# Half of the layer norms offered to GpSimd, and a planner with other transfer times

## The chip, the cores and the metric

The kernel runs on one core of a Trainium2 chip. Its time is the device time of one execution in microseconds (us); several runs give a median. A core has five engines that run their own instruction queues side by side and meet through semaphores: TensorE (PE in the profile, its weight loads PEld), VectorE (DVE), ScalarE (ACT), GpSimd (POOL) and SyncE (SP), which here issues nearly all DMAs.

## The reference, cut to what matters

Two layers, each an attention with a compressive memory (A) and a feed-forward part (B), over 2048 tokens of 640 features in bfloat16. Both layers use the same weights.

```python
def _layernorm(x, axis=-1, eps=1e-05):
    m = jnp.mean(x, axis=axis, keepdims=True)
    v = jnp.var(x, axis=axis, keepdims=True)
    return (x - m) / jnp.sqrt(v + eps)
...
        for s in range(N):                       # N = 4 segments of 512 tokens, H = 32 heads of 20
            qs, ks, vs = (q[:, :, s].copy(), k[:, :, s].copy(), v[:, :, s].copy())
            logits = jnp.einsum('bhqd,bhkd->bhqk', qs, ks) * scale + mask
            p = _softmax(logits, axis=-1)
            a_dot = jnp.einsum('bhqk,bhkd->bhqd', p, vs)
            pq = phi(qs)
            num = jnp.einsum('bhld,bhde->bhle', pq, M)
            den = jnp.einsum('bhld,bhd->bhl', pq, z)[..., None] + 1e-06
            o = g * (num / den) + (1.0 - g) * a_dot
            outs.append(o)
            pk = phi(ks)
            M = M + jnp.einsum('bhld,bhle->bhde', pk, vs)
            z = z + jnp.einsum('bhld->bhd', pk)
...
    x = x + _A_ref(_layernorm(x, axis=-1), A_wq, A_wk, A_wv, A_wo, A_beta)
    x = x + _B_ref(_layernorm(x, axis=-1), B_w1, B_w2)   # relu(x w1) w2, 1728 wide
    x = x + _A_ref(_layernorm(x, axis=-1), A_wq, A_wk, A_wv, A_wo, A_beta)
    x = x + _B_ref(_layernorm(x, axis=-1), B_w1, B_w2)
```

## The kernel before

The residual x stays on the chip (`x_sb`, 16 tiles of 128 tokens). The work is cut by layer a and segment s of four token tiles, written (a,s). For each segment: statistics of each tile on VectorE (`stats`, L729 and L731), variance to reciprocal root on GpSimd (`chain`, the `pow` at L745), the norm itself, which subtracts the mean and multiplies (L775, 128 x 640 to `xn_tok`, two tiles to a slot), and a DMA transposition of each slot (`turn`, L751) to `xnT`. From it K and Q (`proj_part`), V (`proj_v`) or the hidden layer of the feed-forward part (`ffn`) are multiplied by `group`, whose matmuls stand at L708 (128 columns of weights at a time) or L711 (the same as four quarters of 32 columns side by side).

K and Q go through a scratch in DRAM (`spill`, L998, written once, and `fill`, L1042, read as `pad`, with heads spread over rows). The scores of two head groups take five rounds of matmuls (L1226), ScalarE takes their exponentials to `PT` (L1288), GpSimd cuts the part above the diagonal to zero (L1300, the masks), and TensorE multiplies by V (L1320, the value products; L1359 for two of the 64 head groups). The result is cast to `otu`, transposed, divided, added to the memory's part, transposed again to `oT` and multiplied by wo (`out_proj`). The memory itself is written (`mem_write`, L1163) from `phk`, the transposed phi of K, and read at L1106. In the end the sums of the last feed-forward tiles are stored (L1574, L1578).

Nothing of the order is written out by hand. The pieces are generators (streams) that yield operations. A planner, `Sched.run`, keeps a modelled free time for each engine; at each step it takes the stream whose next operation can start first, and records it in its engine's queue. An operation that names two engines goes to the one on which it would end first, as `evac` does for ScalarE and VectorE. The planner's costs are written into the helpers: `dve`, `act`, `pool` for compute, and `issue`, `lat`, `rate` and `holds` for a DMA (the queue's time, time to landing, bytes per ns, and whether SP is taken to stand still until the transfer is done). `SHIFT` moves the modelled start of single pieces, named by stream number and segment, forward or back in that comparison, in ns. None of these numbers is executed: they decide only the order of the queues, and which of two engines gets an operation. The recorded queues are in-order on every engine.

TensorE's array is used in three forms: the full 128 x 128, in four quarters by columns (L711, L1320, L1500) and in four by rows (the scores, L1226). The planner chooses between full and quarters for the operations that offer both, by what stands next to them.

Of the kernel before, what the change touches and what calls it, by code (L numbers as in the profile page):

```python
# [7 lines left out]
ALU = mybir.AluOpType  # L8
# [151 lines left out]
class Spawn:  # L160
# [13 lines left out]
PE_MARGIN = 80.0  # L174
HOLDERS = 1
SHIFT = {
# [8 lines left out]
}  # L185
HOLD_TOL = {"pe": 220.0, "act": 150.0, "dve": 200.0, "pool": 0.0, "sp": 0.0}

# [248 lines left out]
               ("dve", 66.0 + n / (0.96 * mode), [(vfn, True)], 95.0)], waits, urgent=True)  # L436


def pool(ns, fn, waits=()):
    return Op([("pool", ns, [(fn, True)], 60.0)], waits)  # L440

# [7 lines left out]
def bass_interleave_layers__memory_aug_infini_attn__dense_activation_relu__prompt_kernel(  # L449
    nc, A_x, A_wq, A_wk, A_wv, A_wo, A_beta, B_x, B_w1, B_w2, out,  # L450
):
    with contextlib.ExitStack() as es:
# [120 lines left out]
        def late_loads():  # L573

            def x_pieces(s):
                def one(t):
                    return lambda e: e.dma_start(x_sb[:, t, :], xs[:, t, :])
                return [("x%d" % s, 163840, one(4 * s + i)) for i in range(4)]

            def rows(name, w, src, k):  # L580
                return (name, 163840, lambda e: e.dma_start(w[:, k, :], src[128 * k:128 * k + 128, :]))

            def half(k, h):
                cs = slice(h * (DFF // 2), (h + 1) * (DFF // 2))
                return ("w1%d" % h, 221184, lambda e: e.dma_start(w1_r[:, k, cs], B_w1[128 * k:128 * k + 128, cs]))

            pieces = x_pieces(2)
            pieces += [rows("wo", wo_r, A_wo, k) for k in range(FC)]
            pieces += x_pieces(3)
            pieces += [half(k, h) for h in range(2) for k in range(FC)]  # L590
            n2 = len(pieces)
            pieces += [rows("w2", w2_r, B_w2, k) for k in range(NFULL)]
            pieces += [("w2", 81920, lambda e, z=z: e.dma_start(
                w2_r[64 * z:64 * z + DREM, NFULL + z, :], B_w2[NFULL * 128:DFF, :])) for z in range(2)]
            z1 = yield Need("z1")
            sems = {}
            left = {}
            for name, _, _ in pieces:
                left[name] = left.get(name, 0) + 1
            for n, (name, nbytes, fn) in enumerate(pieces):  # L600
                if name not in sems:
                    sems[name] = sem_("d_" + name)
                w = yield Need("ex", *divmod(25 + (n - n2) // 2 if n >= n2 else n * 19 // n2, 5))
                if n == n2:
                    v0 = yield Need("v00")
                    q1 = yield Need("q01")
                    w2w = v0 + q1 + early_done
                tk = yield dma("sp", sems[name], nbytes, fn, w[:1] + (w2w if n >= n2 else []) + z1, issue=400.0, lat=4500.0)
                left[name] -= 1
                if left[name] == 0:  # L610
                    S.set(name, tks=[tk])
# [123 lines left out]
        def chain(t0, n, tk, sq=None):  # L735

            sl = slice(t0, t0 + n)
            if n == 1:
                tk = yield pool(150, lambda e: e.tensor_scalar(lnU[:, sl], mv[:, sl, 1], 1.0, LN_EPS, ALU.mult, ALU.add), tk)
            elif sq is None:  # L740
                tk = yield dve(n, 1, lambda e: e.tensor_scalar(lnU[:, sl], mv[:, sl, 1], LN_EPS, None, ALU.add), tk, port=True)  # L741
            else:
                tk = yield pool(190, lambda e: e.tensor_scalar(lnU[:, sl], sq, 1.0 / D, LN_EPS, ALU.mult, ALU.add), tk)
            h = yield Need("mhalf")
            tk = yield pool(740, lambda e: e.tensor_tensor(rstd[:, sl], lnU[:, sl], mhalf[:, 0:n], ALU.pow), [tk] + h)  # L745
            return tk

        def turn(slot_sem, dst, src, waits):

            n = src.shape[-1] // 128  # L750
            tk = yield dma("sp", slot_sem, 32768 * n, lambda e: e.dma_start_transpose(dst, src), waits,  # L751
                           issue=max(1400.0, 140.0 * n), lat=2400.0, rate=270.0, holds=True)
            return tk

        def lnorm(s, x_tks, slot, p0=0, n=NJ, key=None):
            done = []
            xt = None
            if True:
                aggr = []
                for i in range(p0, p0 + n):  # L760
                    w = []
                    for x in x_tks[i]:
                        t = yield Need(*x)
                        w = w + t
                    tk = yield from stats(4 * s + i, w)
                    aggr.append(tk)
                tch = yield from chain(4 * s + p0, n, aggr)
                if xt is None:
                    xt = yield slot
                    xt = xt[0] if isinstance(xt, list) else xt  # L770
                    if key is not None and p0 == 0:
                        S.set(*key, tks=[xt])
                for i in range(p0, p0 + n, 2):
                    t = 4 * s + i
                    nm = lambda e, bx, t, k: e.tensor_scalar(  # L775
                        bx.ap[:, k * D:k * D + D], x_sb[:, t + k, :], mv[:, t + k, 0:1], rstd[:, t + k:t + k + 1],
                        ALU.subtract, ALU.mult)
                    bx, t0 = yield dve(D, 4, lambda e, bx, t=t: nm(e, bx, t, 0), [tch], extra=120, acq=XN)
                    t1 = yield dve(D, 4, lambda e, bx=bx, t=t: nm(e, bx, t, 1), [tch], extra=120)
                    tT = yield from turn(xn_sem[id(bx)], xt.ap[:, i * FC:(i + 2) * FC, :], bx.ap, [t0, t1] + xt.tks)  # L780
                    bx.release(tT)
                    done.append(tT)
            return xt, done
# [201 lines left out]
        def spill(a, s):  # L985
            for c in range(FC):
                direct = []
                if (a, s) == (0, 0) and c < 2:
                    direct = yield Need("direct", c)
                    if c == 0:  # L990
                        S.set("packed", 0, 0, 0, tks=direct)
                        continue
                ev = []
                for n in range(2):
                    t = yield Need("stg", a, s, c, n)
                    ev = ev + t
                before = S.events.get(("filled", a, s - 2) if s > 1 else ("filled", a - 1, s + 2), [])
                tk = yield dma("sp", scr_sem[s % 2][c], 262144, lambda e, c=c: e.dma_start(  # L998
                    scr[s % 2, 128 * c:128 * c + 128, :], STGS[sx(a, s)][:, c].rearrange("p n t -> p (n t)")),
                    ev + before, issue=350.0, lat=2300.0)  # L1000
                S.set("packed", a, s, c, tks=[tk] + direct)

        def first_heads():
# [25 lines left out]
        def fill(a, s):  # L1029
            got = []  # L1030
            for g in range(0, G, 2):
                if (a, s, g) == (0, 0, 0):
                    yield from first_heads()
                    continue
                sl = yield Acq(PAD)
                w = []
                for c in range(80 * g // 128, (80 * g + 159) // 128 + 1):
                    t = yield Need("packed", a, s, c)
                    w += t
                for hh in range(4):  # L1040
                    src = scr[s % 2, 80 * g:80 * g + 160, :].rearrange("(g h d) t -> d h g t", g=2, d=DH)[:, hh]
                    tk = yield dma("sp", pad_sem[id(sl)], 81920, lambda e, sl=sl, src=src, hh=hh: e.dma_start(  # L1042
                        sl.ap[32 * hh:32 * hh + DH].rearrange("p g n t -> p g (n t)"), src), w + sl.tks, issue=350.0, rate=130.0)
                for z in range(2):
                    S.set("pad", a, s, g + z, tks=[sl, tk])
                got.append(tk)
# [623 lines left out]
```

## Time and profile before

| | |
|---|---|
| median of 3 runs | 557.76 us (557.65 to 559.12) |
| profiled execution, its own time | 557.0 us |
| its span, first to last instruction | 555.0 us |
| PE busy | 543.1 us (98%) |
| DVE busy | 424.5 us (76%) |
| ACT busy | 411.1 us (74%) |
| POOL busy | 193.2 us (35%) |
| chain that ended last, by engine | PE 76%, DVE 15%, DMA 6% |
| norms at L775 | 60 on DVE, mean 561 ns |
| masks at L1300 | 256 on POOL, mean 669 ns |

The spans of a profile are of one execution. A matmul's row is longer than its place in the pipeline, so rows overlap and their ends are modelled; the distance from one start to the next tells what a matmul takes. Idle time of an engine other than the one that sets the end costs nothing by itself.

### The profile page before, as it was taken

The page shows a single profiled execution, that of the slowest core. Times are in us where ns is not written, and L with a number is a line of the kernel's source. Part 1 is how long each engine was busy: PE and PEld are TensorE (multiplying, and loading weights), DVE is VectorE, ACT ScalarE, POOL GpSimd, SP SyncE. Part 2 cuts the span into 40 slices and gives each one's busy share as a digit, 9 for nine tenths or more (in the row PEclk, how much of TensorE's full clock was granted, in tenths as well). Part 3 has the DMA queues.
Part 4 walks back from the last instruction along what each step waited for, and adds up shares of the span by engine and source line. Part 5 has one row for each costly group of instructions (what it writes and reads, how often), then busy time and mean ns, then how long its engine had stood idle before and what let it go on. Part 6 is the DMA issues. An engine that isn't in the chain of part 4 may idle for free.

```text
span 555.0 us, 21258 instructions
## 1 busy us (share of the span) xinstructions
PE 543.1 (98%) x9415; PEld 310.6 (56%) x9415; DVE 424.5 (76%) x1059; ACT 411.1 (74%) x528; POOL 193.2 (35%) x307
## 2 busy tenths in 40 slices
PE   8998999999999999999999999999999999999997
PEld 7643553455664546545556554654645654666766
DVE  4988999998797979896968769987988698427102
ACT  5989888899778877888888757788788878532140
POOL 6334534334344234343433314324444334301000
PEclk9999999999999999999999999999999999999999
DMA  8599899755544263354266344545239712333101
GB/s 272 116 201 210 239 178 220 210 113 132 126 91 88 49 162 68 83 104 90 56 168 107 71 86 143 92 67 90 55 94 164 134 22 49 76 80 62 40 2 51
DMA packets 131907, 61.92 MB, mean 112 GB/s; under 512 B 112136, under 2 KB 121864, under 8 KB 131816
## 3 DMA queue, kind: packets, MB, share of 16 engines
q1 hardware_dynamic: 131384, 60.20, 50.9%
q8 instruction: 74, 1.21, 0.9%
q10 hardware_dynamic: 432, 0.37, 0.2%
q14 instruction: 17, 0.14, 0.1%
HBM read 20.57 MB, written 12.85 MB: 60 GB/s over the span
## 4 chain that ended last, share of the span: by engine, by line
PE 76%; DVE 15%; DMA 6%; ACT 1%; issue 1%; POOL 1%; SPq 0%
PE ps L711 34%; PE ps L708 26%; PE ps L1226 7%; PE ps L1320 5%; DVE stats L729 3%; DVE xn_tok L775 2%; DMA otk<-otu 2%; PE ps L1106 1%; DVE o_sb L1414 1%; DVE x_sb L1546 1%; DVE otu L1330 1%; DMA phk<-phs 1%; DMA oT<-o_sb 1%; PE ps L1163 1%; DMA scr<-w_r 1%
## 5 line engine op out<-in xcount | busy, mean ns | idle before, releaser
L1288 ACT ACTIVATE PT<-ps 128x1024 bf16<-128x1024 f32 x320 | 309.2, 1024 | 59.0 <-PE ps L1226 55.4
L1300 POOL TENSOR_SCALAR_AFFINE_SELECT PT<-PT 128x512 bf16<-128x512 bf16 x256 | 166.5, 669 | 247.1 <-ACT PT L1288 247.1
L711 PE MATMUL ps<-xnT,w_r 128*32 128x512 bf16 x1432 | 88.3, 380 | 0.5 <-DVE hT L1524 0.5
L711 PE MATMUL ps<-w_r,hT 128*32 128x320 bf16 (+1 forms) x1872 | 70.0, 296 | 0.0
L1546 DVE TENSOR_TENSOR x_sb<-x_sb,ps 128x320 bf16<-128x320 bf16 (+1 forms) x65 | 30.9, 475 | 51.0 <-PE ps L711 44.2
L1226 PE MATMUL ps<-pad 20*128 20x512 bf16 (+3 forms) x1024 | 63.4, 301 | 1.5 <-DMA pad<-scr 1.2
L708 PE MATMUL ps<-w_r,hT 128*128 128x320 bf16 x377 | 59.2, 300 | 0.0
L729 DVE BATCH_NORM_STATS2 stats<-x_sb 128x6 f32<-128x320 bf16 x124 | 55.2, 474 | 3.0 <-DMA x_sb<-in_A_x_dram 2.3
L711 PEld LDWEIGHTS ps<-w_r,hT 128*32 128x32 bf16 x1872 | 47.6, 97 | 13.7 <-issue 2.5
L711 PEld LDWEIGHTS ps<-xnT,w_r 128*32 128x32 bf16 x1432 | 35.6, 97 | 32.7 <-issue 4.3
L1525 ACT ACTIVATE hT<-ps 128x512 bf16<-128x512 f32 x55 | 32.8, 599 | 23.5 <-PE ps L711 22.2
L1226 PEld LDWEIGHTS ps<-pad 20*128 20x128 bf16 x1024 | 17.9, 92 | 50.8 <-ACT PT L1288 23.4
L1442 DVE TENSOR_TENSOR x_sb<-x_sb,ps 128x320 bf16<-128x320 bf16 x64 | 30.1, 474 | 20.4 <-PE ps L711 13.8
L708 PEld LDWEIGHTS ps<-w_r,hT 128*128 128x128 bf16 x377 | 34.9, 98 | 17.2 <-issue 4.7
L745 POOL TENSOR_TENSOR rstd<-lnU,mhalf 128x2 f32<-128x2 f32 (+2 forms) x26 | 20.6, 792 | 62.2 <-DVE lnU L741 55.7
L708 PE MATMUL ps<-xnT,w_r 128*128 128x512 bf16 x162 | 40.1, 380 | 0.4 <-issue 0.4
L1320 PE MATMUL ps<-PT,v_aug 128*21 128x128 bf16 (+3 forms) x896 | 40.2, 300 | 0.0
L1524 DVE TENSOR_SCALAR hT<-ps 128x512 bf16<-128x512 f32 x49 | 33.1, 682 | 8.2 <-PE ps L708 6.7
L909 DVE CAST stg<-ps 128x512 bf16<-128x512 f32 (+1 forms) x46 | 30.2, 660 | 6.8 <-PE ps L708 5.9
L1071 ACT ACTIVATE stg<-stg 128x512 bf16<-128x512 bf16 x50 | 31.4, 635 | 4.6 <-DVE rtmp L1069 4.5
L775 DVE TENSOR_SCALAR xn_tok<-x_sb,mv,rstd 128x640 bf16<-128x640 bf16 x60 | 31.9, 561 | 3.7 <-POOL rstd L745 3.5
L1330 DVE CAST otu<-ps 128x512 bf16<-128x512 f32 x48 | 32.6, 680 | 2.6 <-PE ps L1320 1.4
(122 smaller groups left out, 742.3 us busy)
## 6 DMA issues: line engine op xcount, KB each, us to landing
pad<-scr SPq DMA_DIRECT2D x124, 80.0 KB
scr<-stg SPq DMA_DIRECT2D x34, 256.0 KB, 2.6
out_dram<-x_sb SPq DMA_DIRECT2D x15, 160.0 KB, 1.8
w_r<-in_B_w_dram SPq DMA_DIRECT2D x10, 216.0 KB, 3.8
w_r<-in_B_w_dram SPq DMA_DIRECT2D x13, 160.0 KB, 2.9
x_sb<-in_A_x_dram SPq DMA_DIRECT2D x10, 160.0 KB, 3.7
scr<-w_r SPq DMA_DIRECT2D x5, 256.0 KB, 4.4
wk_r<-in_A_wk_dram SPq DMA_DIRECT2D x1, 800.0 KB, 6.8
```

The costliest lines, as they stand in the source:

```text
L708: return e.matmul(view(dst.ap, b), a, b, start=(k == 0), stop=(k == last))
L711: return e.matmul(view(dst.ap[rows], b), part, b, start=(k == 0), stop=(k == last))
L729: tk = yield dve(320, 1, lambda e, c2=c2: e.bn_stats(stats6[:, t, c2, :], x_sb[:, t, c2 * 320:(c2 + 1) * 320]), xt)
L775: nm = lambda e, bx, t, k: e.tensor_scalar(bx.ap[:, k * D:k * D + D], x_sb[:, t + k, :], mv[:, t + k, 0:1], rstd[:, t + k:t + k + 1], ALU. ...
L1226: fns.append([(lambda e, z=z, j=j, hh=hh, N=N, o=o, sl=sl, q=hh % 2: e.matmul(slot.ap[:, q, o:o + N], sl.ap[32 * hh:32 * hh + DH, z, 0, 12 ...
L1288: tx = yield act(1024, lambda e, dst=dst, src=src: e.activation(dst, src, ACT.Exp, scale=SCALE), sc + pw)
L1300: tm = yield pool(600.0, lambda e, reg=reg: e.affine_select(out=reg, in_=reg, pattern=[[0, 4], [1, 128]], compare_op=ALU.is_ge, fill=0.0, ...
L1320: fns.append((lambda e, OD, j=j, hh=hh: e.matmul(OD.ap[32 * hh:32 * hh + DH + 1, 128 * j:L], VAUG[vx(a, s)][:, j, 4 * g + hh, :], pt.ap[:, ...
L1330: te = yield evac(L, 1, lambda e: e.tensor_copy(dst, OD.ap), lambda e: e.activation(dst, OD.ap, ACT.Copy), [tk] + OTU[0].tks)
L1524: th = yield evac(512, 1, lambda e: e.tensor_scalar(hT[:, dc, :], bk.ap[:, :], 0.0, None, ALU.max), lambda e: e.activation(hT[:, dc, :], b ...
L1525: lambda e: e.activation(hT[:, dc, :], bk.ap[:, :], ACT.Relu), [tk] + HT.tks)
L1546: ta = yield dve(n, 1, lambda e: e.tensor_tensor(x_sb[:, t, c0:c0 + n], x_sb[:, t, c0:c0 + n], bk.ap[:, 0:n], ALU.add), [tk], urgent=True)
```

## The change

The two norms of a slot are recorded by a new helper, `both`, that offers VectorE or GpSimd. The second of them gets the slot's earlier transposition among its waits, since it may now be on another engine than the first. The planner's assumed times change for the `pow` (345 ns and 156 for each of its tiles, instead of 740), for the transpositions (which no longer hold SP until they are done), for late loads, the stagings to DRAM and the reads of `pad`. The table `SHIFT` is replaced by another one.

```diff
 SHIFT = {
-    (1, 0): 50, (2, 0): 800, (7, 2): 1550, (7, 6): -2850, (8, 1): -350, (8, 6): -200, (8, 7): 1500, (9, 3): -850,
...
+    (1, 0): 750, (2, 0): 50, (10, 4): 300, (10, 5): -3300, (11, 1): -150, (11, 5): 800, (11, 6): -600,
...
 }
+def both(n, mode, fn, waits=(), extra=0.0, acq=None):
+    return Op([("dve", 66.0 + n / (0.96 * mode) + extra, [(fn, True)], 95.0),
+               ("pool", 54.0 + n / 0.96, [(fn, True)], 60.0)], waits, acq=acq, port=True)
...
-                tk = yield dma("sp", sems[name], nbytes, fn, w[:1] + (w2w if n >= n2 else []) + z1, issue=400.0, lat=4500.0)
+                tk = yield dma("sp", sems[name], nbytes, fn, w[:1] + (w2w if n >= n2 else []) + z1, issue=540.0, lat=2400.0, rate=345.0)
...
-            tk = yield pool(740, lambda e: e.tensor_tensor(rstd[:, sl], lnU[:, sl], mhalf[:, 0:n], ALU.pow), [tk] + h)
+            tk = yield pool(345.0 + 156.0 * n, lambda e: e.tensor_tensor(rstd[:, sl], lnU[:, sl], mhalf[:, 0:n], ALU.pow), [tk] + h)
...
-                           issue=max(1400.0, 140.0 * n), lat=2400.0, rate=270.0, holds=True)
+                           issue=max(1560.0, 140.0 * n), lat=2300.0, rate=285.0)
...
-                    bx, t0 = yield dve(D, 4, lambda e, bx, t=t: nm(e, bx, t, 0), [tch], extra=120, acq=XN)
-                    t1 = yield dve(D, 4, lambda e, bx=bx, t=t: nm(e, bx, t, 1), [tch], extra=120)
+                    bx, t0 = yield both(D, 4, lambda e, bx, t=t: nm(e, bx, t, 0), [tch], extra=120, acq=XN)
+                    t1 = yield both(D, 4, lambda e, bx=bx, t=t: nm(e, bx, t, 1), [tch] + bx.tks, extra=120)
...
-                    ev + before, issue=350.0, lat=2300.0)
+                    ev + before, issue=480.0, lat=1700.0, rate=345.0)
...
-                        sl.ap[32 * hh:32 * hh + DH].rearrange("p g n t -> p g (n t)"), src), w + sl.tks, issue=350.0, rate=130.0)
+                        sl.ap[32 * hh:32 * hh + DH].rearrange("p g n t -> p g (n t)"), src), w + sl.tks, issue=420.0, lat=1700.0, rate=135.0)
```

In the order that comes out, 30 of the 60 norms stand on GpSimd. VectorE has 1023 instructions instead of 1059, GpSimd 30 more than before, ScalarE 6 more (evacuations). Nearly every queue is reordered: with other assumed times and shifts, K, Q and V of several segments, memory writes and reads and out projections stand at other places among the scores.

15 rows, old and new, of the table SHIFT are left out of this document.

## The prediction

> **What bounds the kernel now.** I read the page first, then the busy time by stretch, the groups by form, TensorE's timeline around its gaps, and the waits.
>
> ```profile
> span 555.0 us, 21258 instructions
> PE 543.1 (98%) x9415; PEld 310.6 (56%) x9415; DVE 424.5 (76%) x1059; ACT 411.1 (74%) x528; POOL 193.2 (35%) x307
> ```
> ```profile
> 0.00:14.00 14.00, 11.96 (x114) 9.93 (x115) 6.44 (x18) 7.89 (x19) 8.58 (x28) 1.00 0.80 270
> 14.00:70.00 56.00, 51.83 (x629) 28.86 (x627) 50.10 (x135) 50.57 (x69) 24.13 (x36) 1.00 0.84 190
> 70.00:520.00 450.00, 447.37 (x7837) 250.22 (x7839) 362.92 (x896) 344.51 (x429) 160.52 (x244) 1.00 0.51 103
> 520.00:555.00 35.00, 31.94 (x848) 21.58 (x840) 5.04 (x11) 8.14 (x14) 0.00 (x0) 1.00 0.09 29
> ```
>
> In the second fence the first number after the comma is TensorE's busy time. It is idle for 2.0 us in the start, 4.2 us from 14 to 70, 2.6 us in the 450 us of the middle and 3.1 us in the last 35 us (the last matmuls and the store behind them). So TensorE sets the time, at a granted clock of 1.00 throughout. The change doesn't take work off TensorE; it can only move gaps.
>
> A busy PE may still hide gaps, since a matmul's row is longer than the spacing to the next. These rows give the spacing:
>
> ```profile
> 264.72 0.84 PE L708 MATMUL ps<-wv_r,xnT 128*128 128x320 bf16 x5
> 265.39 0.84 PE L708 MATMUL ps<-wo_r,oT 128*128 128x320 bf16 x5
> 266.17 0.40 PE L1226 MATMUL ps<-pad 20*128 20x384 bf16 x8
> ```
>
> Five matmuls of 320 columns go from 264.72 to 265.39: 0.135 us each, 0.42 ns a column. The next five would be done at 266.06 and the scores (another tile form of the array) start at 266.17: 0.10 us for a change of form. With these two prices I counted the order of before: all its matmuls and its 320 changes of form make 533.5 us. The last matmul row stands at 551.7 (quoted below), the first at about 1.5, so some 17 us of the 550 are gaps, the start's included.
>
> **TensorE's own stream.** The new order has the same matmuls, but 296 of the full 128-wide ones are now recorded as four quarters side by side, which is why its PE count rises by 888.
>
> ```profile
> L711 PE MATMUL ps<-xnT,w_r 128*32 128x512 bf16 x1432 | 88.3, 380 | 0.5 <-DVE hT L1524 0.5
> L708 PE MATMUL ps<-xnT,w_r 128*128 128x512 bf16 x162 | 40.1, 380 | 0.4 <-issue 0.4
> ```
>
> Four quarters take 4 x 88.3/1432 = 0.247 us, one full matmul 40.1/162 = 0.248 us: no difference, 296 x 0.001 = 0.3 us at most, taken as nothing. Changes of form go from 320 to 323: +0.3 us. So the counted stream is 533.5 us before and 533.8 after.
>
> **Gaps that end with a DMA.** Four in before are large enough to name:
>
> ```profile
> 31.06 0.84 PE L708 MATMUL ps<-wv_r,hT 128*128 128x320 bf16 x5
> 33.13 0.40 PE L1226 MATMUL ps<-pad 20*128 20x512 bf16 x4 [1.23 <-DMA pad<-scr]
> ...
> 48.51 1.25 PE L708 MATMUL ps<-hT,wk_r 128*128 128x512 bf16 x5
> 50.60 0.29 PE L1163 MATMUL ps<-w_r,phk 128*128 128x147 bf16 x2 [0.84 <-DVE w_r L909]
> ...
> 371.60 0.82 PE L711 MATMUL ps<-xnT,w_r 128*32 128x512 bf16 x12
> 372.85 0.39 PE L1163 MATMUL ps<-v_aug,phk 128*32 128x147 bf16 x12 [0.42 <-DMA phk<-phs]
> ...
> 386.36 0.58 PE L708 MATMUL ps<-wv_r,xnT 128*128 128x320 bf16 x3
> 387.63 0.44 PE L708 MATMUL ps<-wo_r,oT 128*128 128x320 bf16 x2 [0.69 <-DMA oT<-o_sb]
> ```
>
> By the spacing the gaps are 33.13 - 31.06 - 5 x 0.135 - 0.10 = 1.29; 50.60 - 48.51 - 5 x 0.217 = 1.00; 0.60; and 0.86 us. The second is put down to a cast, but the same instruction also needs `phk`, whose transposition was issued here:
>
> ```profile
> 45.37 1.24 SPq L751 DMA_TRANSPOSE phk<-phs  x1
> DMA to landing us min/median/max: 3.1/3.9/5.7
> ```
>
> 45.37 plus 3.1 to 5.7 is 48.5 to 51.1, which holds the 50.5 at which it starts. Now the new order, with matmul work between producer and consumer as the measure of room:
> - First memory write of segment (0,0), second part: from the last K matmul it reads to the write there were 19.5 us of matmul work and it took 23.7; the new order has 46.9 us. The 1.00 goes.
> - Memory write (1,2): 51.3 us of work before, 80.5 after. The 0.60 goes.
> - Out projection of (1,1): from the segment's last value matmul 14.5 us of work, it took 16.0; now 27.2. The 0.86 goes. The other segments keep 13.3 to 15.6, one 46.6 (before, 11.7, 12.6, 13.4 and 14.1 us left no gap), and the first 7.75 against 5.85.
> - The `pad` fill at 33.13 has 9.12 us of work where it had 9.40 (0.28 later), but SP issues it ahead of one x load of 0.43 us that it stood behind: 0.15 us better. Bounds: the whole 1.29 goes, or it grows to 1.6.
> - The first w1 matmul of (0,0) keeps its 10.1 us of work: no change.
>
> ```profile
> 27.12 0.43 SPq L577 DMA_DIRECT2D x_sb<-in_A_x_dram  x1
> 27.59 1.93 SPq L1042 DMA_DIRECT2D pad<-scr  x4
> ```
>
> Sum: -1.00 - 0.60 - 0.86 - 0.15 = -2.6 us. Bounds: -3.8 (the pad's too), and 0, if other transfers come late by as much in the new order.
>
> **Gaps that end with an evacuation (a PSUM bank comes free late).**
>
> ```profile
> PE ps L711 <- DVE otu L1330: 1.0, 2, 0.6
> PE ps L708 <- DVE w_r L909: 0.7, 1, 0.7
> PE ps L711 <- DVE hT L1524: 0.5, 1, 0.5
> PE ps L711 <- ACT w_r L910: 0.4, 1, 0.4
> ```
>
> 2.6 us in five waits; each row shows its idle less the modelled tail of 0.38 - 0.21 = 0.17 us, so 3.4 us. In the order of before 42 hand-overs from a VectorE evacuation to a matmul have under 1.4 us of matmul work between the source matmul and the one that waits; in the new order 26. Under 1.0 us it is 18 and 7. Scaled so, the 3.4 us fall by 1.3 to 2.1; I take -1.7. Bounds: -3.4 and 0.
>
> **The norms themselves.** 30 of the 60 at L775 go from DVE to POOL.
>
> ```profile
> L775 DVE TENSOR_SCALAR xn_tok<-x_sb,mv,rstd x60: 342/442/832, 20.6 to 508.1; 128x640 bf16<-128x640 bf16 x60
> L775 DVE TENSOR_SCALAR xn_tok<-x_sb,mv,rstd 128x640 bf16<-128x640 bf16 x60 | 31.9, 561 | 3.7 <-POOL rstd L745 3.5 <-DMA xnT<-xn_tok 0.2
> L1300 POOL TENSOR_SCALAR_AFFINE_SELECT PT<-PT x256: 628/634/1031, 20.6 to 481.4; 128x512 bf16<-128x512 bf16 x128
> L1288 ACT ACTIVATE PT<-ps 128x1024 bf16<-128x1024 f32 x320 | 309.2, 1024 | 59.0 <-PE ps L1226 55.4 <-PE ps L1320 2.9
> ```
>
> DVE loses 30 x 0.561 = 16.8 us of its 424.5. POOL's price for 640 elements isn't in the trace; the masks do 512 in 0.634, so 0.63 to 1.03 (the slowest mask), by size 0.634 x 640/512 = 0.79, which I take: POOL gains 24 us on 193. Neither engine sets the end, so the direct price is nothing: at the segments after the start, 10 us and more of matmul work lie between the last sum that a norm needs and the first matmul that reads it, and that hides a norm that is 0.4 us slower. If that cover were gone, a segment would cost 0.79 - 0.56 = 0.23 us. The rows also show what the two engines do to each other: a norm takes 342 ns or up to 832, a mask 628 or up to 1031.
>
> [...]
>
> **The masks** that queue behind the norms are where the change can cost TensorE. A norm on POOL waits for its `pow` and, as `both` has it, for the last transposition from its slot; behind it on POOL stand masks, and for those the value products wait (the transposition behind each pair of norms stays on SP). A value product waits for the last mask; from the last score matmul that takes two exponentials (2 x 1.024) and two masks (2 x 0.634) and about 0.1, that is 3.42 us, with one mask 2.84. The new order leaves 3.0, 3.4 and 3.8 us of matmul work at value products 3, 5 and 11 (of 64 head groups, in order), where before had 5.0, 4.1 and 4.3, and 3.9 to 4.2 at nine more. At product 3 a `pow` and at 11 and 19 a norm stands among the three POOL instructions ahead of the last mask. So 0.42 us at product 3 without the `pow`, 0.4 more with it, 0.1 at the others: +0.9. Bounds: +0.4, and +4.2 if a norm of 0.79 stood in every such place.
>
> **Sum:** +0.3 - 2.6 - 1.7 + 0.9 = -3.1 us. The profiled execution took 557.0 us (span 555.0), 0.8 under the median of 557.76; from the median it gives 554.7 us. About 0.3% (1.7 us) is what a measurement of this kernel can tell from no change.
>
> The end of the kernel doesn't move: its last matmuls, residual sums and stores are recorded as before, within 0.5 us of matmul work.
>
> ```profile
> 551.70 0.24 PE L711 MATMUL ps<-w_r,hR 128*32 128x160 bf16 x4
> 552.34 0.35 ACTq L1574 DMA_DIRECT2D out_dram<-x_sb  x1
> ```
>
> **Rivals.** (1) All named gaps go and the new ones stay small: -3.8 - 3.4 + 0.4 + 0.3 = -6.5, 551.3 us; if the 4.2 us idle of 14 to 70 halve as well, 549.2. For it: more work at nearly every long hand-over. Against it: 56 us at the start in which DVE and ACT are both 90% busy. [...] (3) POOL becomes late for the masks: each norm runs 0.79 us and stands before the last mask at the dozen products with 3.0 to 4.2 us of room. Then the masks cost 4.2 us, the bank gain is 0, and 0.3 - 2.6 + 4.2 = +1.9 gives 559.7; at the 1.03 us of the slowest mask it would be 8.5 and 564. It decides once more than half of these places have a norm ahead; the order shows three or four. (4) The start: K and Q of segments (0,1) and (0,2) come 11 to 16 us of matmul work earlier, and with them SP's stagings stand between the loads. If the 4.2 us idle of 14 to 70 double, the sum is +1.1, 558.9, no change; triple, 563.
>
> **Chances.** Forecast 0.48 (554.7; its own range 552.5 to 556.5, a tenth of it inside no change); rival 1 0.17; rival 2 0.12; rival 3 0.13; rival 4 0.10, two thirds of it slower. Faster by over 0.3%: 0.43 + 0.17 = 0.60. Slower: 0.13 + 0.07 = 0.20. Within: 0.05 + 0.12 + 0.03 = 0.20. For 8 in 10 the range goes from rival 1's far end, 549, to rival 3's nearer price, 560.
>
> **What would show it.** In the new numbering the lines stand six further down. Right: PE idle from 14 to 520 below the 6.8 us of now; no gap at L1169 (the memory write) that ends with `phk`; 30 POOL norms at L781 of 0.7 to 0.9 us; DVE busy near 407. Wrong: value products (L1326) waiting for POOL by more than 3 us in total, more than 6 us idle from 14 to 70, or gaps of 1 us that end with `xnT` or `oT`.

## The result: 582.22 us against 557.70, slower by 4.4%

The changed kernel took 582.22 us (median of 4 runs, 580.27 to 583.58), the kernel before 557.70 (4 runs, 557.34 to 559.12). The ratio is 1.0442 (95% interval 1.0408 to 1.0477). The forecast was 554.7 us, its range 549 to 560. The profiled execution took 583.58 us, with a span of 581.8.

The page of the kernel after:

```profile
span 581.8 us, 23066 instructions
PE 551.9 (95%) x10303; PEld 314.3 (54%) x10303; DVE 411.1 (71%) x1023; ACT 413.8 (71%) x534; POOL 272.0 (47%) x337
PEclk9999998989998999999999999979999999999999
PE 70%; POOL 13%; DVE 6%; ACT 4%; DMA 4%; issue 1%; SPq 1%
```

The same line of the chain that ended last, for the kernel before:

```profile
PE 76%; DVE 15%; DMA 6%; ACT 1%; issue 1%; POOL 1%; SPq 0%
```

POOL had 1% of that chain and now has 13%, and the clock that was granted to TensorE is under full speed in four slices. Busy time by stretch of the kernel after (PE, PEld, DVE, ACT, POOL, then clock, DMA share and GB/s):

```profile
14.00:70.00 56.00, 53.52 (x624) 26.87 (x622) 48.72 (x121) 52.56 (x69) 30.63 (x41) 1.00 0.91 211
70.00:520.00 450.00, 427.75 (x8013) 237.62 (x8016) 337.91 (x843) 339.97 (x425) 228.55 (x266) 0.98 0.49 97
```

From 14 to 70 us the kernel is better than before (2.5 us idle where there were 4.2). The loss lies in the middle, where TensorE was idle for 2.6 us and is now idle for 22.3. The norms, as the view of their line in the kernel after has them (minimum, median and maximum in ns, first and last start in us):

```profile
L781 DVE TENSOR_SCALAR xn_tok<-x_sb,mv,rstd x30: 342/448/995, 20.6 to 537.4; 128x640 bf16<-128x640 bf16 x30
L781 POOL TENSOR_SCALAR xn_tok<-x_sb,mv,rstd x30: 2493/2541/3363, 21.2 to 536.4; 128x640 bf16<-128x640 bf16 x30
```

The same operation on the same shape takes 0.45 us on VectorE and 2.54 us on GpSimd. What TensorE waits for in the kernel after (us in total, times, longest):

```profile
PE ps L1326 <- POOL PT L1306: 16.5, 9, 3.7
PE ps L714 <- DMA w_r<-in_B_w_dram: 1.9, 1, 1.9
PE ps L714 <- issue: 1.8, 1, 1.8
PE ps L1169 <- DMA phk<-phs: 1.4, 1, 1.4
```

Nine value products wait for masks. Before, TensorE's list had no such row for its matmuls; only seven weight loads of value products waited for masks, 1.5 us in all. Two places show how it comes about. From GpSimd's timeline, first the norm of the slot that is read at 92.87, then the norms and masks ahead of the second longest of the nine waits; below them TensorE's side of both:

```profile
86.48 2.74 POOL L781 TENSOR_SCALAR xn_tok<-x_sb,mv,rstd 128x640 bf16<-128x640 bf16 x1
...
294.93 7.85 POOL L781 TENSOR_SCALAR xn_tok<-x_sb,mv,rstd 128x640 bf16<-128x640 bf16 x3
302.74 2.98 POOL L1306 TENSOR_SCALAR_AFFINE_SELECT PT<-PT 128x512 bf16<-128x512 bf16 x5
```

```profile
92.87 0.38 PE L714 MATMUL ps<-xnT,w_r 128*128 128x512 bf16 x1 [1.81 <-issue]
...
300.65 0.31 PE L717 MATMUL ps<-w_r,hR 128*32 128x320 bf16 x4
304.01 0.72 PE L1326 MATMUL ps<-PT,v_aug 128*21 128x512 bf16 x16 [3.04 <-POOL PT L1306]
```

Three norms hold GpSimd for 7.85 us from 294.93. Five masks are queued behind them and start at 302.74; the value product that needs the second of them starts at 304.01, after 3.04 us of idle time. The planner had counted 3 x 0.72 us for these norms. The gap before 92.87 is a reader of `xnT`: the GpSimd norm of that slot starts at 86.48 and ends at 89.22, and the transposition behind it is issued at 89.30.

With 0.17 us for the modelled tail of the row ahead of each gap, the nine gaps at value products are about 18 us (16.5 + 9 x 0.17) of the 26.8 by which the span grew. What the rest is, the experiments have to tell.

### The profile page after: what moved, and what is told of

It reads as the page before. It is cut to its first block, busy times and chain, and to the rows that moved or that the text cites. A ratio compares the mean times of both kernels' runs of the same rounds, so it can differ in the third digit from the quotient of the medians.

```text
span 581.8 us, 23066 instructions
## 1 busy us (share of the span) xinstructions
PE 551.9 (95%) x10303; PEld 314.3 (54%) x10303; DVE 411.1 (71%) x1023; ACT 413.8 (71%) x534; POOL 272.0 (47%) x337
## 4 chain that ended last, share of the span: by engine, by line
PE 70%; POOL 13%; DVE 6%; ACT 4%; DMA 4%; issue 1%; SPq 1%
PE ps L717 39%; PE ps L714 17%; POOL xn_tok L781 9%; PE ps L1232 6%; PE ps L1326 5%; ACT PT L1294 4%; POOL PT L1306 3%; DVE stats L735 2%; DMA phk<-phs 2%; PE ps L1112 1%; PE ps L1169 1%; POOL rstd L751 1%; DMA pad<-scr 1%; DVE x_sb L1448 1%; DMA oT<-o_sb 1%
## 5 line engine op out<-in xcount | busy, mean ns | idle before, releaser
L717 PE MATMUL ps<-xnT,w_r 128*32 128x512 bf16 x1848 | 117.9, 386 | 0.2 <-DMA xnT<-xn_tok 0.2
L781 POOL TENSOR_SCALAR xn_tok<-x_sb,mv,rstd 128x640 bf16<-128x640 bf16 x30 | 79.2, 2644 | 0.5
L717 PEld LDWEIGHTS ps<-xnT,w_r 128*32 128x32 bf16 x1848 | 45.0, 98 | 44.6 <-issue 10.1
L717 PE MATMUL ps<-w_r,hT 128*32 128x320 bf16 (+1 forms) x1812 | 68.3, 296 | 0.0
L714 PE MATMUL ps<-w_r,hT 128*128 128x320 bf16 x392 | 64.4, 306 | 1.9 <-DMA w_r<-in_B_w_dram 1.9
L1326 PE MATMUL ps<-PT,v_aug 128*21 128x128 bf16 (+3 forms) x896 | 41.3, 305 | 16.5 <-POOL PT L1306 16.5
L1530 DVE TENSOR_SCALAR hT<-ps 128x512 bf16<-128x512 f32 x55 | 37.6, 687 | 19.3 <-PE ps L717 15.3
L1531 ACT ACTIVATE hT<-ps 128x512 bf16<-128x512 f32 x49 | 29.2, 599 | 28.1 <-PE ps L717 27.3
L714 PEld LDWEIGHTS ps<-w_r,hT 128*128 128x128 bf16 x392 | 36.6, 99 | 21.6 <-issue 5.5
L1326 PEld LDWEIGHTS ps<-PT,v_aug 128*21 128x21 bf16 x896 | 21.9, 93 | 37.5 <-POOL PT L1306 20.7
L1420 DVE TENSOR_TENSOR o_sb<-otk,rden 128x320 bf16<-128x320 bf16 x62 | 34.7, 588 | 0.4
```

The source lines that it names most:

```text
L714: return e.matmul(view(dst.ap, b), a, b, start=(k == 0), stop=(k == last))
L717: return e.matmul(view(dst.ap[rows], b), part, b, start=(k == 0), stop=(k == last))
L781: nm = lambda e, bx, t, k: e.tensor_scalar(bx.ap[:, k * D:k * D + D], x_sb[:, t + k, :], mv[:, t + k, 0:1], rstd[:, t + k:t + k + 1], ALU. ...
L1326: fns.append((lambda e, OD, j=j, hh=hh: e.matmul(OD.ap[32 * hh:32 * hh + DH + 1, 128 * j:L], VAUG[vx(a, s)][:, j, 4 * g + hh, :], pt.ap[:, ...
L1420: to = yield dve(320, 1, lambda e, z=z, dst=dst: e.tensor_tensor(dst, av[:, z, :, :, 0:DH], rd.ap[:, z].to_broadcast([128, NJ, 4, DH]), AL ...
L1530: th = yield evac(512, 1, lambda e: e.tensor_scalar(hT[:, dc, :], bk.ap[:, :], 0.0, None, ALU.max), lambda e: e.activation(hT[:, dc, :], b ...
```

## The experiments

Two theories stood at the start. The first: the order is no worse than planned, and the slow norm on GpSimd, which keeps the masks back, is the whole loss. The second: the order itself (shifts and assumed times) costs the time, or the two engines hinder each other. Where a run is compared, "before" means the runs of the kernel before beside it. Each edit moves the line numbers a little; the names of the tiles stay.

**The order of after with all norms on VectorE.** The planner decides and records as in the changed kernel, but what it gives to GpSimd of the norms goes to VectorE's queue, at its place in the order. The queues of TensorE, ScalarE and SyncE are those of after.

```diff
-            self.P.waits(e, waits)
+            q = "dve" if e == "pool" and len(op.alts) == 2 else e
+            self.P.waits(q, waits)
...
-                    tk = self.P.op(e, fn, mark)
+                    tk = self.P.op(q, fn, mark)
```

> The recorded order of after on TensorE, ScalarE and SyncE, word for word; only the 30 norms that its planner gave to GpSimd are executed by VectorE, each at its place in the recorded order. Late masks (theory A: a norm holds GpSimd for 2.5 us, the masks behind it come late, value products wait 16.5 us and the clock halves for 17 us): the waits of the value products for GpSimd fall from 16.5 us to under 3, the granted clock returns to 1.00, and the time is 552 to 560 us. The new order itself (theory B: other shifts and transfer times leave TensorE without work): TensorE's gaps stay and the time is 574 us or more.

Measured: 555.48 us (6 runs) against 557.07 (9 runs), ratio 0.9954 (0.9934 to 0.9973). The page, busy time by stretch and TensorE's two longest waits behind the start:

```profile
span 553.7 us, 23048 instructions
PE 542.3 (98%) x10303; PEld 314.2 (57%) x10303; DVE 416.9 (75%) x1053; ACT 413.8 (75%) x534; POOL 194.9 (35%) x307
```
```profile
14.00:70.00 56.00, 52.83 (x621) 26.89 (x619) 48.68 (x122) 52.00 (x69) 24.72 (x37) 1.00 0.94 207
70.00:520.00 450.00, 447.25 (x8773) 257.13 (x8774) 356.92 (x906) 345.95 (x435) 161.37 (x242) 1.00 0.52 102
```
```profile
PE ps L1170 <- DMA phk<-phs: 1.9, 1, 1.9
...
PE ps L715 <- DVE w_r L916: 1.2, 1, 1.2
```

In TensorE's list no matmul waits for GpSimd any more, and the clock is 1.00 throughout. So the order is not the loss: by itself it is a small gain, 0.3 to 0.7%, and this version is faster than both kernels. Everything over 555.5 comes from where the norms of this order run.

**The same, with a stand-in of the norm's length on GpSimd.** As above, and at each place where after had a norm on GpSimd (but the first), GpSimd computes a `pow` over 14 numbers that nobody reads.

```diff
+                    if q != e and ("maskg",) in self.events:
...
+                        self.stood.append(self.P.op("pool", self.standin(k % 6), True))
...
+        S.standin = lambda k: lambda e: e.tensor_tensor(gtf[:, 14 * k:14 * k + 14], sval[:].to_broadcast([128, 14]),
+                                              mhalf[:, 0:1].to_broadcast([128, 14]), ALU.pow)
```

> As the run above (norms executed by VectorE, same order), but at each place of a norm in GpSimd's queue, the first at 21 us excepted, GpSimd runs a stand-in: a pow over 14 numbers, by the price of the pow rows 345 + 156 x 14 = 2.5 us, whose result nobody reads. It tells late masks from late norms. If it is the masks behind (A): value products wait for GpSimd as in after, 14 to 20 us, and the time is 574 to 584. If it is the norms' own consumers that come late (their transpositions and the matmuls behind them): those are on time here, and the time is 553 to 561.

Measured: 574.54 us (4 runs), ratio 1.0319 (1.0285 to 1.0353). The stand-in among GpSimd's groups, and TensorE's longest wait:

```profile
L524 POOL TENSOR_TENSOR gt<-sval,mhalf 128x14 f32<-128x14 f32 x29 | 75.7, 2630 | 0.0
```
```profile
PE ps L1337 <- POOL PT L1317: 16.1, 8, 3.5
```

An instruction over 14 numbers, whose result nobody reads, brings back 19.1 of the 26.7 us between the first experiment and after, with nearly the same wait at the value products (16.1 us where after has 16.5) and a clock of 0.988. So for these 19.1 us it is time in GpSimd's queue ahead of the masks that costs, not what the norm reads or writes.

**The length varied.** The stand-in with 3 and with 8 numbers instead of 14: 0.93 and 1.69 us in the mean.

> The order of after with all norms executed by VectorE, and stand-ins on GpSimd of the length that the prediction assumed for a norm: a pow over 3 numbers, 345 + 156 x 3 = 0.81 us. The prediction put the cost for the masks at 0.9 us (0.4 to 4.2) at that length. If its reading of the room at the value products was right and only the length was wrong, the time is within 2 us of the 555.5 of the run without stand-ins; if the room was misread as well, it is 560 or more.

> The same with a pow over 8 numbers, 345 + 156 x 8 = 1.59 us. Between 0.81 and 2.53 us a wait grows by what exceeds the room, in chains of two or three norms by a multiple of it: value products wait 3 to 7 us, no stretch of 3.41 us loses half of it, so the clock stays at 1.00: 558 to 564 us. If it were only the number of instructions on GpSimd that counted, it would be as slow as with 2.53 us, 574.

Measured: 555.26 us (12 runs) against 557.12 (23 runs), ratio 0.9959 (0.9935 to 0.9982), and 556.61 (10 runs), 0.998 (0.9959 to 1.0). With the short one no value product waits for GpSimd; with the middle one two do:

```profile
PE ps L1337 <- POOL PT L1317: 1.2, 2, 0.9
```

So at a length even a little over the one that I had assumed the masks would have cost nothing. The cost is far from linear: about nothing at 0.93 us, 1.1 us at 1.69, 19.1 us at 2.63. The 1.1 us are not clear of noise, since the intervals of the two ratios overlap. The middle one missed its expectation of 558 to 564 us on the mild side.

**What the norm costs on GpSimd by itself.** The kernel before, with six forms of instruction three times each at the end of GpSimd's queue, on dead tiles.

```diff
+            (640, lambda e, o: e.tensor_scalar(o, src, mhalf[:, 0:1], mhalf[:, 1:2], ALU.subtract, ALU.mult)),
+            (640, lambda e, o: e.tensor_scalar(o, src, 0.5, 2.0, ALU.subtract, ALU.mult)),
+            (640, lambda e, o: e.tensor_scalar(o, src, mhalf[:, 0:1], None, ALU.mult)),
+            (320, lambda e, o: e.tensor_scalar(o, src[:, 0:320], mhalf[:, 0:1], mhalf[:, 1:2], ALU.subtract, ALU.mult)),
+            (640, lambda e, o: e.tensor_copy(o, src)),
+            (512, lambda e, o: e.affine_select(...)),
```

> Before, with 18 more GpSimd instructions behind its last pow, on tiles that nobody reads any more: three times the norm's form (subtract, multiply, two per-partition scalars, 640 elements), the same with immediate numbers, with one scalar and one operation, with 320 elements, a copy of 640, and a mask of 512. The time stays at 557. [...]

One run, 557.05 us; GpSimd's timeline, in the order of the diff (the first of three rounds; the other two agree within 0.02 us):

```profile
508.07 2.51 POOL L1641 TENSOR_SCALAR stg<-wk_r,mhalf 128x640 bf16<-128x640 bf16 x1
510.55 2.35 POOL L1642 TENSOR_SCALAR stg<-wk_r 128x640 bf16<-128x640 bf16 x1
512.89 1.89 POOL L1643 TENSOR_SCALAR stg<-wk_r,mhalf 128x640 bf16<-128x640 bf16 x1
514.77 1.45 POOL L1644 TENSOR_SCALAR stg<-wk_r,mhalf 128x320 bf16<-128x320 bf16 x1
516.16 0.72 POOL L1645 COPY stg<-wk_r 128x640 bf16<-128x640 bf16 x1
516.83 0.64 POOL L1646 TENSOR_SCALAR_AFFINE_SELECT stg<-stg 128x512 bf16<-128x512 bf16 x1
```

The form of the norm takes 2.51 us with no mask or `pow` around it and VectorE busy for 7.9 of the 25 us from 505 to 530. From the two lengths, 2.51 - 1.45 = 1.06 for 320 elements is 3.3 ns an element, and 0.39 us is left as fixed (an estimate from these two rows). A copy of 640 takes 0.72 and a mask of 512 takes 0.64. It is the kind of instruction, not the neighbours. On the masks' row, whose operation has TENSOR_SCALAR in its name too, my price was built.

**The waits filled.** After, with 11, 4, 11, 8 and 14 matmuls that nobody reads put ahead of five of the late value products (numbers 20, 27, 37, 41 and 47), to keep TensorE at work while it waits.

```diff
+FILLERS = {20: 11, 27: 4, 37: 11, 41: 8, 47: 14}
...
+            prod.pre = [lambda e, OD: e.matmul(OD.ap[:, :], wk_r[:, 0, 0:128], wk_r[:, 0, 0:512], start=True, stop=True)
+                        ] * FILLERS.get(n, 0)
```

> After, with matmuls that nobody reads (512 columns, 0.22 us each) put on TensorE into the same PSUM bank ahead of the mask wait of five value products: 11, 4, 11, 8 and 14 of them at products 20, 27, 37, 41 and 47, less than each gap. The waits stay, only TensorE isn't idle in them. If the clock follows TensorE's activity in fixed stretches of 3.41 us, the three half-speed stretches that follow these products (179.1, 380.5 and 383.9 us in the trace of after) go, those after the gaps at 90 and 121 us stay, the granted clock rises from 0.985 to about 0.994, and the time falls by 3 to 5 us to 577 to 580. If the clock drops for another reason, nothing moves.

Measured: 576.53 us (4 runs) against 557.54 (7 runs), ratio 1.0366 (1.0323 to 1.0409). Span and clock, and the wait that is left:

```profile
core 0: 575.2 us, clock 0.997
```
```profile
PE ps L1332 <- POOL PT L1312: 6.3, 9, 1.1
```

48 needless matmuls make the kernel faster than after, by 5.7 us in the medians and by 0.8%, some 4 us, in the ratios, whose intervals just touch. The clock goes with it: in the four runs of after its mean is 0.985 to 0.991, here 0.994 to 1.000, and 1% of 580 us is 5.8. Of the five half-speed stretches that the trace of after shows, the three behind the filled waits are gone. A fourth, behind the wait for w2 weights at 123.48, is gone too, but not by the fillers: that wait was 1.2 us in this execution where it was 1.9. So most of the gain is the part of the loss which isn't waiting but running slowly behind a wait.

**The planner told the true price.** After, with 2540 ns in place of 721 for a norm on GpSimd; and the order of that with its ten norms executed by VectorE (this edit and that of the first experiment together).

```diff
-               ("pool", 54.0 + n / 0.96, [(fn, True)], 60.0)], waits, acq=acq, port=True)
+               ("pool", 2540.0, [(fn, True)], 60.0)], waits, acq=acq, port=True)
```

> After with one number changed: the planner's price of a norm on GpSimd is 2540 ns, the median that the trace of after shows, instead of 721. It then records 10 norms on GpSimd, and orders all queues anew. A: value products wait for GpSimd under 3 us and the time is 551 to 559. B: the shifts and transfer times are the cause, and it stays at 570 or more.

> The order that the planner makes with the price of 2540 ns, but its 10 GpSimd norms are executed by VectorE. The run with that price took 566.0 us. If the ten norms cost what is left (late masks, VectorE held up), the time falls to 552 to 558; if the order itself is bad (the shifts were fitted to another one), it stays at 562 to 567.

Measured: 565.98 us, ratio 1.0172 (1.013 to 1.0215), and 567.76, ratio 1.0196 (1.0162 to 1.0231). The true price takes 20 of the 30 norms off GpSimd and 16 us off the time, but the result is still slower than before; it lies between the two outcomes expected, 551 to 559 and 570 or more. It isn't the ten norms: without them the time is no better (567.76, just over the 562 to 567 expected if the order is bad). TensorE's longest waits with the true price, first with the ten norms on GpSimd and then on VectorE:

```profile
PE ps L1112 <- DVE om_sb L1127: 2.8, 3, 1.4
PE ps L1232 <- ACT PT L1294: 2.0, 4, 0.7
```
```profile
PE ps L1113 <- DVE om_sb L1128: 2.8, 3, 1.4
PE ps L1233 <- ACT PT L1295: 2.3, 6, 0.7
```

These are waits for evacuations and exponentials, and nearly the same in both; all waits of value products for masks in the run with the ten norms come to 0.2 us. So it is the order that is worse. That the shifts stand at the wrong places in it is my reading: no run takes the shifts apart from the transfer times.

**The shifts and times without the norms' choice.** After with `dve` for both norms, planned anew.

```diff
-                    bx, t0 = yield both(D, 4, lambda e, bx, t=t: nm(e, bx, t, 0), [tch], extra=120, acq=XN)
-                    t1 = yield both(D, 4, lambda e, bx=bx, t=t: nm(e, bx, t, 1), [tch] + bx.tks, extra=120)
+                    bx, t0 = yield dve(D, 4, lambda e, bx, t=t: nm(e, bx, t, 0), [tch], extra=120, acq=XN)
+                    t1 = yield dve(D, 4, lambda e, bx=bx, t=t: nm(e, bx, t, 1), [tch], extra=120)
```

> After without `both`: all norms recorded on VectorE, the new transfer times and the new shifts kept, so the planner makes another order. If nothing but GpSimd's norms is wrong in the change, 552 to 560 us. If the shifts hold only for the one order they were fitted to, 560 to 570, as with the true price.

Measured: 569.19 us, ratio 1.0223 (1.0199 to 1.0248), where the first experiment, with the same norms on the same engine but in the order planned for the choice, took 555.48. The new shifts and times were run in three orders, and in one of them they are a gain.

**The choice alone.** Before with `both` and its two uses, the old shifts and times.

> Before, with `both` alone: old transfer times, old shifts, the price of 721 ns. The planner records 31 norms on GpSimd. If the price is the cause, value products wait for GpSimd by 10 us or more and the time is 572 to 592; if the new shifts or transfer times are, it stays at 555 to 562.

Measured: 613.88 us, ratio 1.1027 (1.0995 to 1.1058), with 31 norms on GpSimd. TensorE's longest waits:

```profile
PE ps L1325 <- POOL PT L1305: 16.7, 6, 5.5
PE ps L1168 <- DMA phk<-phs: 6.4, 3, 3.9
PE ps L1364 <- POOL PT L1305: 4.6, 1, 4.6
```

The masks are late here too, by 21.3 us in two lines, as the price would have it, but the time is far over the 572 to 592 expected: other waits come on top, and the mean clock is 0.964 where after has 0.985. How much of the 56 us is the engine and how much the order was not taken apart.

## Why the prediction was wrong, point by point

**The step that failed** is the price of a norm on GpSimd: 0.79 us, with 1.03 as the upper end, "by size" from the masks' row. It is 2.64 us in the mean. Two errors stand in it: the masks are another kind of instruction, and the upper end of the bounds was taken from the slowest instance of that other kind, which bounds nothing. The ratio of the two engines' medians in after is 2541/448 = 5.7.

**The masks' term** (+0.9, bounds +0.4 to +4.2) hangs on that price and is the term that was mis-sized: about 18 us of waits, and the slow clock behind them. Its mechanism was named rightly, and also that the norms queue ahead of masks. The room at the value products (3.0 to 4.2 us) was not read too large: with 0.93 us in place of 0.79 no wait for a mask is listed, where the sum had 0.9, and with 1.69 us it is 1.2. I asked of that room only what an instruction of 0.8 us would do. With the short stand-in the time is 555.26 us, close to the 554.7 forecast, but partly by luck: the masks' +0.9 came to nothing, and the banks' -1.7 is not seen either.

**The direct price, put at nothing,** failed too, on a smaller scale. The 10 us and more of matmul work behind a norm were to hide one that is 0.4 us slower. A norm that is 2.1 us slower was not hidden at 92.87, where TensorE stood for 1.8 us.

**Rival 3** (GpSimd late for the masks, chance 0.13) is what happened, at nine value products instead of a dozen, with 559.7 to 564 us as its price. Both ends were worked out with a norm of 1.03 us at most; and a dozen norms longer by 0.24 us add 2.9 to the 4.2, which makes 7.1, so the 8.5 of the far end does not follow from the places named. Its condition, a norm ahead at more than half of the places, was the wrong test: three norms in a row at one place cost 3 us.

**The clock** was in no term. I took 1.00 as given because the trace of before shows nothing else. In after five stretches of 3.41 us run at 0.50, which costs up to 1.7 us each. The run with the fillers has one left and takes 5.7 us less.

**The order's terms** (+0.3 - 2.6 - 1.7 = -4.0) had the right sign and two fifths to two thirds of the size: the first experiment is faster by 0.46%, that is 2.6 us of 557.07, and by 1.6 us in the medians. In it the gaps of `phk` in (1,2) and of `oT` in (1,1) are gone from the list of waits, and the one of `pad` at 33 us is 0.29 us where it was 1.23, better than the 0.15 that I had granted. The `phk` gap in the second part of (0,0), for which I counted 46.9 us of room, went as well: those eight matmuls start without a listed wait, at 81.69 in the first experiment and at 80.49 in after. But a new one came ahead of the first part of the same write, which had none at 39.99 before: 1.9 us at 73.49 in the first experiment and 1.4 at 72.19 in after. That part was in none of my terms. In after its transposition was issued at 63.40, 8.8 us ahead of the write, and the longest of the twelve landings took 8.7 us, where their median is 4.0; why, the rows don't tell. So matmul work between producer and consumer was no sufficient measure of room, since one landing took twice the median.

The banks, -1.7, stay half open: the waits for evacuations that the list names, 2.6 us before, are 2.4 in the first experiment, where VectorE has the norms back, so the order alone didn't bring it. In after they are 0.9, which would be the term's size, but there TensorE stands at the masks meanwhile, and the runs don't separate the two.

**Steps that held:** no price for quarters against full matmuls (PE is busy for 542.3 us in the first experiment, 543.1 before, with 888 more instructions); the start, where rival 4's trouble did not come; VectorE relieved, 411.1 us against about 407 named.

**The ledger** of after against the first experiment is 26.7 us. The stand-in accounts for 19.1, waits and slow clock together. For part of the other 7.7 the rows give a place: the late `xnT` at 92.87, 1.8 us; the w2 weights, 1.9 us where the first experiment has 0.3; and a mean clock of 0.985 against the stand-in's 0.988, some 1.7 us (an estimate: 0.003 of the span). The w2 weights are not read by a norm, but their loads stand in SyncE's queue behind a transposition to `xnT` that is issued at 107.34, when a GpSimd norm ends at 107.26: the first of the loads is issued at 111.11, and at 105.86 in the first experiment. The remaining 2 to 3 us I did not take apart.

## What to carry to other kernels

Before an operation is offered to a second engine, that very form is to be measured there; a row of another kind of instruction, however alike its name, gave neither the price nor a bound here (0.79 us, at most 1.03, against 2.54 measured). An engine that looks a third busy can still be the wrong place, when what is queued behind the newcomer has only a few us of room. And a planner's table of offsets may be worth something in one order alone: here the new shifts and times together were a small gain in one order, and a loss in the two that came out at another price or without the choice.

## What the runs showed of the hardware that I had not expected

**In after the clock was halved on a grid of 3.41 us.** Its stretches at half speed start at 94.08, 124.80, 179.41, 380.80 and 384.21 us and are 3.41 us long each; the starts lie 9, 16, 59 and 1 times 3.413 us apart. Windows on that grid (PE busy time first, the clock third from the end):

```profile
90.67:94.08 3.41, 1.60 (x24) 0.60 (x26) 1.64 (x5) 1.58 (x4) 1.22 (x2) 1.00 1.04 195
94.08:97.49 3.41, 3.41 (x40) 1.20 (x28) 3.19 (x7) 1.90 (x3) 1.64 (x2) 0.50 0.92 50
298.87:302.28 3.41, 2.10 (x30) 1.03 (x27) 0.76 (x2) 2.60 (x3) 3.41 (x2) 1.00 0.32 70
302.28:305.70 3.42, 1.69 (x52) 1.26 (x56) 0.91 (x2) 0.14 (x1) 3.42 (x6) 1.00 0.80 151
305.70:309.11 3.41, 3.41 (x42) 1.87 (x35) 1.27 (x4) 1.94 (x2) 0.67 (x3) 1.00 0.77 148
333.00:336.41 3.41, 1.62 (x36) 0.79 (x40) 0.85 (x2) 0.41 (x1) 3.41 (x6) 1.00 0.52 97
336.41:339.82 3.41, 3.03 (x25) 1.23 (x21) 1.67 (x3) 1.94 (x2) 1.16 (x3) 1.00 1.12 213
377.38:380.79 3.41, 0.95 (x28) 0.49 (x20) 1.45 (x6) 1.18 (x2) 3.41 (x3) 1.00 0.00 0
380.79:384.20 3.41, 2.15 (x29) 0.85 (x30) 0.00 (x0) 0.65 (x2) 2.97 (x6) 0.50 0.61 130
384.20:387.62 3.42, 3.42 (x15) 1.95 (x14) 0.00 (x0) 1.88 (x2) 1.22 (x2) 0.50 0.92 162
```

The stretch with 1.81 us idle (90.67 to 94.08) is followed by one at 0.50. The wait of 3.04 us that ends at 304.01 lies across two stretches, with 1.31 and 1.73 us idle in them, and leaves the clock alone, though it is longer than the 1.81 us that halved it at 92.87. The two cases lie close together in these rows, whose matmul ends are modelled: 1.79 us idle (333.00 to 336.41) left the clock alone. The stretch from 380.79 ran at half speed with 1.26 us idle, and the one behind it at half speed too, though 1.79 us idle in a stretch at full speed had no such effect at 333.00. What went with the clock at full speed in these rows was the idle time within one stretch of the grid, not the length of a wait.

**A VectorE norm was not held for the length of a GpSimd norm.** The DVE norm of the same slot runs inside the POOL norm quoted at 86.48, as VectorE's timeline has it:

```profile
86.58 0.44 DVE L781 TENSOR_SCALAR xn_tok<-x_sb,mv,rstd 128x640 bf16<-128x640 bf16 x1
```

It takes its usual 0.44 us while GpSimd is busy from 86.48 to 89.22. The slowest VectorE norm took 0.995 us and the slowest on GpSimd 3.36 against 2.49 at best, so in these durations whatever the two do to each other is under a microsecond.
